# One written-out order exchanged for another: same transfers, other engines for the copies, more 64 by 64 transposes, half the zero products

## The chip, the cores and the metric

The kernel runs on one core of a Trainium2 chip. The metric is the device time of one execution in microseconds (us). TensorE (PE in the profile) multiplies matrices and transposes; its weight loads have a row of their own (PEld). VectorE (DVE), ScalarE (ACT) and GpSimd (POOL) do the elementwise work, and the queues of SyncE (SP), ScalarE and GpSimd issue the transfers (DMA). Each engine executes its own instructions in program order and waits on semaphores for the others.

## The reference

A retention layer (linear attention with a decay per head) is followed by a WaveMLP-like block. B = 4 batches, H = 8 heads, S = 768 tokens, D = 64, so the model width is 512.

```python
for t in range(S):
    state = gamma[None, :, None, None] * state + np.einsum('bhd,bhe->bhde', k[:, :, t], v[:, :, t])
    y[:, :, t] = scale * np.einsum('bhd,bhde->bhe', q[:, :, t], state)
# x = y with the heads side by side: (B, S, 512)
theta = x @ w_theta
zr, zi = x * cos(theta), x * sin(theta)
u = x + einsum('ts,bsd->btd', w_tok_r, zr) + einsum('ts,bsd->btd', w_tok_i, zi)
out = u + maximum(u @ w_ch, 0)
```

## The kernel before

The work is cut into small named steps, and one list, `ORDER`, says in which order they are emitted. A token such as `ck.7.p` calls step `ck` for unit 7 with engine `p` (`p` GpSimd, `v` VectorE, `a` ScalarE, and for transfers `s` the SP queue, `a` the ACT queue). Each engine gets its instructions in the order of the list; `tc.manual_schedule()` leaves that order alone and adds the semaphores. No planner runs in the kernel.

**Retention, 24 units.** Unit n is one half of the heads (4) in one block of 256 tokens; three blocks make a batch, so units come in pairs and six make a batch. `Lk`, `Lq`, `Lv` load 256 KB each. `ck` casts k to bf16, `cq` or `cqs` casts q or also scales it, `cv` scales v. `Tk` and `Tq` transpose with four 128 by 128 products each into one PSUM bank, and `E` copies the bank out. Their second form, `Tk6`, `Tq6` and `E6`, uses sixteen 64 by 64 products each, writes two PSUM banks (both buffers of tag `tr`) and copies them out in two halves. A third form, `Dk`, is a DMA transpose from the SP queue. `A` makes the scores (sixteen products in 64 by 64 mode), `m` masks them on VectorE, `Y` multiplies them with v. `ST` makes the state's increment, `S0` and `S1` add it up, `SB` casts the state's two halves into a block-diagonal tile, and `I` multiplies it with q. `XB` (a cast on any engine) or `XA` (a product with the decay, on VectorE) brings the result out, depending on whether q was scaled before.

**The block after it, 24 tiles of 128 tokens.** `Tx` and `Ex` (or `Tx6` and `Ex6`, or the DMA transpose `Dx`) turn x back. `Hh` multiplies with w_theta, `CN` takes cosine or sine on ScalarE, `z` multiplies both with x. `Tw` and `Ew` (or `Tw6`, `Ew6`) transpose the token weights, whose rows `Pw` loads from the GpSimd queue in three groups for each of the two matrices (`Pw.1.1` is the second group of w_tok_i, rows 128 to 383). `M.t.s` is one pair of products of 512 columns of output tile t, `u` adds x, `Tu`, `Tu6` or `Du` transposes, `O` multiplies with w_ch, `f` closes, `SO` stores. `Mh`, `uh`, `Tuh`, `Euh`, `Oh`, `fh` are the last tile in halves.

**Zero products and constants.** `Z.n` is two products of 128 by 512 on a zero tile into a spare PSUM bank; nothing reads them, and n only makes the token unique. `const1` clears that tile on VectorE, `const6` clears the block-diagonal tiles, `const2`, `const4`, `const5`, `constA` set up positions, identity and mask on GpSimd, `const3`, `const8`, `const9` make the decay tables on ScalarE, `const7` switches its table to sine.

The lines where the two kinds of transpose differ:

```python
for x in range(4):                                      # kq_half: L318
    nc.tensor.transpose(st["kq_ps", n][:, 4 * w + x, :],
                        st["kqb", n][:, w, x * P:(x + 1) * P], K["ident"])
...
for c in range(2):                                      # tiles64: L337
    for r in range(2):
        rows = slice(r * D, (r + 1) * D)
        nc.tensor.transpose(ps[r][c * D:(c + 1) * D, x, :],
                            src[rows, x * P + c * D:x * P + (c + 1) * D],
                            K["ident"][rows, rows])
```

Of the kernel before, what the change touches and what calls it, by code (L numbers as in the profile page):

```python
# [32 lines left out]
Ex.2.v S0.5.v z.0.p Tq.6 E.6.a CN.2.0 cv.6.p Hh.3 SB.5.0.v Tx.3 Tw.1.0 z.1.v SB.5.1.a Ew.1.0.v Ex.3.a
CN.2.1 A.6 I.5 Y.5 ST.6 XA.5.0 z.2.v Tw.0.0 CN.3.0 Tx.4 CN.3.1 Ew.0.0.v S0.6.v XA.5.1 Ex.4.v Hh.4 CN.4.0
CN.4.1 Tw.0.1 M.0.1 Pw.1.1 z.3.v M.0.0 Tw.0.2 Pw.1.2 Ew.0.2.a SB.6.1.a Hh.5 z.4.p SB.6.0.p Lk.9.a M.0.3
ck.7.p cqs.7.p M.0.2 CN.5.1 CN.5.0 cq.8.v m.6 Ew.0.1.v Tw.1.1 Tw.1.2 Ew.1.1.v Lv.9.s M.0.4 M.1.0 Tx.5
Ew.1.2.v M.1.1 S1.6 Tk.7 M.1.4 Pch Ex.5.v z.5.v cv.7.v Tq.8 Tq.7 M.1.2 E.7.a M.0.5 I.6 Y.6 ST.7 A.7
ck.8.a u.0 S0.7.v m.7 XA.6.1 SB.7.1.a M.1.5 M.1.3 XA.6.0 Tw.1.3 M.2.5 Pw.0.2 M.2.3 u.1 S1.7 Tk.8 M.2.1
M.2.0 SB.7.0.v Ew.1.3.a Tu.0 I.7 cv.8.v E.8.a Lk.10.s cv.9.p Y.7 ST.8 A.8 cqs.9.v ck.9.v M.2.4 Du.1
Eu.0.a XB.7.1.a XB.7.0.v S0.8.v SB.8.0.v M.2.2 Tx.6 Tq.9 Tk.9 Lv.10.a ck.10.p cv.10.p Lq.10.s S1.8 u.2  # L40
m.8 O.0 E.9.a SB.8.1.a Hh.6 Tw.1.4 I.8 Y.8 A.9 CN.6.0 Du.2 Lq.14.s CN.6.1 Ex.6.v f.0 ST.9 Tw.0.3 Hh.7
Ew.1.4.v Ew.0.3.a S0.9.v Tw.0.4 M.3.0 CN.7.0 CN.7.1 M.3.2 Dx.7 M.3.1 M.3.5 M.3.3 Lv.11.s Lk.11.s XA.8.1
Ew.0.4.v Lq.11.s M.3.4 S1.9 u.3 Tw.0.5 Tk.10 M.4.5 cqs.10.p XA.8.0 m.9 M.4.3 Tq.10 SB.9.1.a SB.9.0.a I.9
O.2 Lq.12.s Lk.12.s E.10.a Lk.15.s Ew.0.5.v Lk.14.s Y.9 ST.10 Tw6.1.5 Ew6.1.5.0.a Ew6.1.5.1.a A.10 z.7.p
Lv.12.s XB.9.1.a XB.9.0.a f.2 M.4.0 O.1 M.4.1 cq.11.a ck.11.p cqs.14.p m.10 f.1 S0.10.v ck.12.v M.4.4
M.4.2 Tu.3 Eu.3.a Dk.11 Dx.9 SB.10.0.a cqs.12.p u.4 Hh.9 z.6.v ck.15.v M.5.0 M.5.4 SB.10.1.p cv.11.p
M.5.2 M.5.3 I.10 M.5.5 M.5.1 Lq.13.a Tu6.4 A.11 Y.10 ck.14.v ST.11 CN.9.1 CN.9.0 SO.0.a Eu6.4.1.a Hh.8
u.5 Eu6.4.0.v S0.11.v XB.10.0.a m.11 Dk.12 Tx.8 O.4 Lv.13.a SB.11.0.a Lq.15.s Lk.13.s XB.10.1.a CN.8.1
Lk.18.a CN.8.0 SB.11.1.p cv.12.p Lq.16.s I.11 Ex.8.v Y.11 Tk6.14 Tq6.14 ST.12 f.4 E6.14.0.v E6.14.1.a
Lv.15.s O.3 z.8.p XA.11.0 XA.11.1 Hh.10 A.12 S0.12.a f.3 z.9.v SB.12.0.v Tx.10 CN.10.1 Dx.11 Ex.10.v  # L50
Lk.16.s Lv.17.s Hh.11 SO.2.s CN.10.0 m.12 S1.12 z.10.v cq.13.v M.6.1 M.6.2 M.6.0 M.6.3 CN.11.0 CN.11.1
M.7.3 SB.12.1.a Lk.17.a ck.13.a M.7.4 M.7.0 M.6.4 Dk.13 M.7.1 z.11.v SO.3.s A.14 Tu6.5 M.6.5 Eu6.5.0.a
Eu6.5.1.a M.7.2 I.12 Lv.14.s u.6 cqs.15.v M.7.5 M.9.3 ck.17.a m.14 SO.4.a Lq.17.s Lq.18.s Lk.21.s
ck.16.a M.9.0 M.9.5 M.9.1 M.9.4 Lq.19.a M.9.2 Du.6 cv.13.v u.7 u.9 Y.12 cv.14.p ST.13 Tk6.15 Tq6.15
E6.15.0.v E6.15.1.v A.13 O.5 XB.12.1.a XB.12.0.a M.8.1 S0.13.a S1.13 M.8.4 M.8.3 SB.13.0.a SB.13.1.p
cq.16.p m.13 I.13 ck.18.a Y.13 ST.14 A.15 M.8.0 f.5 cq.17.v Lv.18.a M.8.5 M.8.2 XA.13.0 XA.13.1 S0.14.v
SB.14.0.p Lv.16.s Hh.13 S1.14 u.8 M.10.1 cv.15.p cv.17.p SB.14.1.p M.10.0 M.10.4 cqs.18.v M.10.5 CN.13.0
CN.13.1 Hh.12 CN.12.1 I.14 m.15 Y.14 CN.12.0 ST.15 S0.15.v XB.14.1.a SB.15.0.a M.10.3 cv.16.v Dk.16
Dk.17 Du.7 Dx.13 M.10.2 Dk.18 O.6 SB.15.1.p XB.14.0.v S1.15 I.15 Y.15 ST.16 Tx6.12 SO.5.a cv.18.p f.6
S0.16.v A.16 M.11.4 cq.19.p SB.16.1.p M.11.1 Lq.21.a Ex6.12.0.a Ex6.12.1.a z.12.p SB.16.0.a Lk.19.s  # L60
Lk.20.s XB.15.0.a u.10 z.13.p XB.15.1.a m.16 O.7 Du.10 I.16 Y.16 Tu6.8 ST.17 f.7 Eu6.8.0.v Eu6.8.1.a
A.17 Hh.15 CN.15.1 CN.15.0 Dx.14 M.11.2 Tx.15 Lv.22.s SO.7.s M.11.0 M.11.5 S0.17.v SB.17.0.p M.11.3
XA.16.1 m.17 XA.16.0 Ex.15.v Hh.14 SB.17.1.p z.15.p ck.21.p ck.19.p I.17 u.11 Tu6.11 A.18 Y.17 ST.18
Eu6.11.1.v S0.18.v XA.17.1 XA.17.0 O.10 SO.1.a S1.18 Lv.19.a CN.14.1 CN.14.0 Dx.16 Lq.20.a f.10 Lq.22.a
SB.18.0.a Hh.17 Eu6.11.0.a SB.18.1.a I.18 Tk.19 Tq.19 CN.17.1 O.8 CN.17.0 m.18 E.19.a Hh.16 z.14.p
Lv.20.s Du.9 f.8 O.11 Y.18 cv.19.p ck.20.a CN.16.1 ST.19 A.19 Tx6.17 CN.16.0 M.12.1 f.11 Ex6.17.0.v
Ex6.17.1.v cq.20.p Lk.22.s Dk.20 M.12.0 S0.19.a M.13.3 M.13.2 XB.18.1.a SB.19.1.p SB.19.0.v M.13.0
z.17.v cqs.21.v XB.18.0.v S1.19 z.16.v m.19 cv.20.v M.12.3 M.12.2 M.13.5 Lv.21.s M.13.1 M.12.4 M.12.5
I.19 M.13.4 Y.19 ST.20 u.12 A.20 Dk.21 XA.19.1 S0.20.v XA.19.0 ck.22.a cq.22.a SB.20.1.p cv.22.p M.14.3
M.14.5 M.14.1 M.14.4 M.14.2 M.14.0 SB.20.0.p u.13 m.20 S1.20 Hh.19 I.20 Y.20 SO.10.s Lq.23.s Lk.23.s  # L70
cv.21.v u.14 A.21 ST.21 CN.19.0 CN.19.1 S0.21.v M.15.3 M.15.5 S1.21 m.21 XA.20.1 Hh.18 CN.18.1 CN.18.0
Dx.18 Dk.22 ck.23.a M.15.4 M.15.2 SB.21.0.p M.15.1 M.15.0 SB.21.1.v Lv.23.s Du.12 Dx.19 XA.20.0 O.9 f.9
I.21 Y.21 A.22 ST.22 M.16.1 cqs.23.p u.15 m.22 S0.22.v z.18.p z.19.p M.16.5 SB.22.0.p M.16.4 O.12 M.16.0
SO.8.a M.16.2 M.16.3 SB.22.1.p XB.21.0.a XB.21.1.a SO.11.s Du.14 cv.23.p Dk.23 f.12 Du.13 Dx.20 Dx.21
Hh.21 u.16 I.22 A.23 Y.22 ST.23 CN.21.0 CN.21.1 Hh.20 CN.20.1 S0.23.v XA.22.1 XA.22.0 SB.23.0.a M.17.1
M.17.3 CN.20.0 M.17.0 SB.23.1.p I.23 M.17.2 m.23 Y.23 O.13 M.17.4 z.21.v M.17.5 Mh.0.1 Mh.0.3 XB.23.1.v
f.13 Hh.23 u.17 XB.23.0.a SO.13.a CN.23.1 Du.16 Hh.22 z.20.v CN.22.1 Mh.0.2 M.19.3 Dx.23 CN.23.0 Dx.22
# [628 lines left out]
```

## Time and profile before

| | us |
|---|---|
| median of three runs | 164.74 (164.14 to 164.97) |
| span of the profiled execution, first to last instruction | 163.3 |
| TensorE busy | 154.7 (95%) |
| VectorE busy | 114.5 (70%) |
| ScalarE busy | 78.8 (48%) |
| GpSimd busy | 74.3 (45%) |

The profiled execution is known by its span; the device time of the runs also holds what lies before the first and after the last instruction, here 1.4 us between the span and the median. Busy times are sums over the span. TensorE's products are pipelined: one of 512 columns is listed with 380 ns, and the next starts 216 ns after it, so starts are read rather than durations.

### The profile page before, as it was taken

To read this page: it belongs to the slowest core of one execution; us is meant where nothing else is said; L and a number is where in the kernel's file an instruction comes from. 1 tells how busy PE (TensorE), PEld (TensorE's weight loads), DVE (VectorE), ACT (ScalarE), POOL (GpSimd) and SP (SyncE) were. 2 spreads that over 40 slices of the span, in tenths; PEclk is the share of its full clock that TensorE was granted. 3 is DMA by queue.
4 is the path that set the end of the run, shared out by engine and by line. 5 is a ranking of instruction groups with operands and counts; after the bars stand their busy time and mean duration, and the time that the engine had idled before them with its cause. 6 is when DMAs were issued, how large, how long until landed. Compare 5 with 4: busy or idle time off the path is not lost.

```text
span 163.3 us, 5070 instructions
## 1 busy us (share of the span) xinstructions
PE 154.7 (95%) x2100; PEld 85.5 (52%) x2100; DVE 114.5 (70%) x217; ACT 78.8 (48%) x147; POOL 74.3 (45%) x106
## 2 busy tenths in 40 slices
...
DMA  4999999999999999999999999999896527514446
GB/s 116 297 290 252 258 294 240 277 220 285 226 162 275 296 205 220 251 207 245 335 236 172 242 195 305 222 192 276 185 251 129 101 64 225 161 68 128 128 156 230
DMA packets 70118, 35.19 MB, mean 215 GB/s; under 512 B 27472, under 2 KB 67152, under 8 KB 70096
## 3 DMA queue, kind: packets, MB, share of 16 engines
...
q0 software_dynamic: 2688, 3.41, 12.1%
...
## 4 chain that ended last, share of the span: by engine, by line
PE 79%; DMA 7%; DVE 6%; POOL 4%; issue 1%; ACT 1%; DVEq 0%; POOLq 0%
PE y_ps L559 33%; PE o_ps L595 10%; PE th_ps L511 10%; PE zz L279 5%; PE r_ps L458 4%; PE at_ps L380 4%; DMA x_sb<-xT 4%; DMA kqT<-kqb 3%; PE kq_ps L318 3%; PE w_ps L533 2%; DVE at L389 2%; POOL z L525 2%; PE r_ps L446 2%; PE y_ps L620 2%; PE r_ps L408 1%
## 5 line engine op out<-in xcount | busy, mean ns | idle before, releaser
L559 PE MATMUL y_ps<-z,wtr 128*128 128x512 bf16 x138 | 52.4, 380 | 0.0
L559 PE MATMUL y_ps<-z,wti 128*128 128x512 bf16 x138 | 52.3, 379 | 0.0
L525 POOL TENSOR_TENSOR z<-cs,x_sb 128x1024 bf16<-128x1024 bf16 x12 | 25.5, 2135 | 17.7 <-ACT cs L518 10.8
L389 DVE TENSOR_TENSOR at<-at_ps,mask 128x1024 bf16<-128x1024 f32 x24 | 29.2, 1215 | 0.5 <-PE at_ps L380 0.5
L310 POOL TENSOR_TENSOR vb<-vf,vsc 128x512 bf16<-128x512 f32 x15 | 15.6, 1045 | 21.7 <-ACT sbd L136 11.7
L601 DVE SCALAR_TENSOR_TENSOR ot<-o_ps,u 128x512 f32<-128x512 f32 x22 | 15.1, 688 | 13.6 <-PE o_ps L595 13.5
L511 PE MATMUL th_ps<-wth,xT 128*128 128x512 bf16 x96 | 24.5, 380 | 0.0
L566 DVE TENSOR_TENSOR u<-y_ps,x_sb 128x512 bf16<-128x512 f32 x23 | 15.8, 688 | 10.9 <-PE y_ps L559 10.5
L595 PE MATMUL o_ps<-wch,uT 128*128 128x512 bf16 x88 | 22.6, 380 | 0.0
L518 ACT ACTIVATE cs<-th_ps,halfpi 128x512 bf16<-128x512 f32 x24 | 16.3, 682 | 11.8 <-PE th_ps L511 7.0
L518 ACT ACTIVATE cs<-th_ps,zerob 128x512 bf16<-128x512 f32 x24 | 16.4, 684 | 10.6 <-PE th_ps L511 5.1
L559 PEld LDWEIGHTS <-wtr 128*128 128x128 bf16 x138 | 13.5, 98 | 13.4
L559 PEld LDWEIGHTS <-wti 128*128 128x128 bf16 x138 | 13.5, 98 | 12.7 <-issue 0.4
L138 POOL CAST sbd<-s 64x256 bf16<-64x256 f32 (+1 forms) x20 | 8.4, 418 | 24.3 <-DVE s L426 22.1
L136 ACT COPY kqT<-kq_ps 128x1024 bf16<-128x1024 bf16 (+1 forms) x10 | 9.7, 969 | 9.8 <-PE kq_ps L318 9.5
L511 PEld LDWEIGHTS <-xT 128*128 128x128 bf16 x96 | 8.7, 98 | 8.5
L279 PE MATMUL zz<-zero 128*128 128x512 bf16 x30 | 10.8, 495 | 1.9 <-DVE zero L191 1.9
L595 PEld LDWEIGHTS <-uT 128*128 128x128 bf16 x88 | 8.1, 98 | 8.4 <-issue 0.2
L136 ACT CAST kqb<-kqf 128x512 bf16<-128x512 f32 x16 | 9.6, 620 | 5.5 <-DMA kqf<-in_k_dram 5.4
L458 PE MATMUL r_ps<-at,vb 64*64 64x128 bf16 x384 | 10.0, 221 | 1.6 <-DVE at L389 1.6
L380 PE MATMUL at_ps<-kqT 64*64 64x128 bf16 x384 | 10.0, 220 | 1.1 <-DVE kqT L138 0.6
L476 DVE TENSOR_TENSOR xT<-r_ps,qx 128x256 bf16<-128x256 f32 x22 | 8.7, 417 | 1.8 <-PE r_ps L458 0.8
...
## 6 DMA issues: line engine op xcount, KB each, us to landing
vf<-in_v_dram SPq DMA_DIRECT2D x20, 256.0 KB, 5.7
kqf<-in_k_dram SPq DMA_DIRECT2D x19, 256.0 KB, 5.4
kqf<-in_q_dram SPq DMA_DIRECT2D x17, 256.0 KB, 5.7
out_dram<-ot ACTq DMA_DIRECT2D x12, 256.0 KB, 2.5
out_dram<-ot SPq DMA_DIRECT2D x11, 256.0 KB, 2.4
kqf<-in_q_dram ACTq DMA_DIRECT2D x7, 256.0 KB, 5.4
kqf<-in_k_dram ACTq DMA_DIRECT2D x5, 256.0 KB, 6.7
vf<-in_v_dram ACTq DMA_DIRECT2D x4, 256.0 KB, 5.7
```

The costliest lines, as they stand in the source:

```text
L136: nc.scalar.copy(dst, src)
L279: nc.tensor.matmul(t[:m, :cols], K["zero"][:, :m], K["zero"][:, :cols], start=True, stop=True)
L310: engines[e].tensor_mul(in_blocks(vb), by_token(raw["vf", n]), _bcast_last(K["vsc"][:, i, :, h * HU:(h + 1) * HU], D))
L380: nc.tensor.matmul(at_ps[cols, g, j, a, :], kq_at(n, 0, a, j, c)[rows], kq_at(n, 1, slice(0, 2), j, c)[rows], start=(j == 0 and a == 0), s ...
L389: nc.vector.tensor_mul(at.rearrange("p g j a t -> p (g j) (a t)"), st["at_ps", n].rearrange("p g j a t -> p (g j) (a t)"), _bcast_mid(K["m ...
L458: nc.tensor.matmul(st["R", n + 1][c][g * D:(g + 1) * D, j * P:(j + 1) * P], st["vb", n][rows, lo:lo + D], st["at", n][rows, g, j, a, :], s ...
L511: nc.tensor.matmul(th_ps, st["xT", C][:, j, :], K["wth"][:, j, :], start=(j == 0), stop=(j == 3))
L518: nc.scalar.activation(st["cs", C][:, w, :], st["th_ps", C], AF.Sin, bias=K["zerob" if w else "halfpi"], scale=1.0)
L525: engines[e].tensor_mul(st["z", b][:, c], st["cs", C], _bcast_mid(x_of(C), 2))
L559: nc.tensor.matmul(st["y", t], K["wT"][r][:, s0, t0 * P:(t0 + 1) * P], st["z", b][:, s0, r, :], start=(done == 0 and r == 0), stop=(done = ...
L566: nc.vector.tensor_add(st["u", t], st["y", t], st["x", b][:, t0, :])
L595: nc.tensor.matmul(o_ps, st["uT", t][:, j, :], K["wch"][:, j, :], start=(j == 0), stop=(j == nD - 1))
```

## The change

Only `ORDER` is exchanged; no function and no tile is changed. All transfers (`Lk`, `Lq`, `Lv`, `Pth`, `Pch`, `Pw`, `Dk`, `Dx`, `Du`, `SO`, `SOh`) stand in the same order in both lists, on the same queues. The constants' order and the place of every compute step between the transfers are new. Of the steps that may run on several engines, many name another one: of the 24 `z`, GpSimd had 12 and has 3 now. In the second form instead of the first are now `Tk`/`Tq` of units 0, 1, 2, 8 and 19, `Tw.0.3`, `Tw.1.4`, `Tx.8` and `Tx.15` with their copies. Units 7, 10, 14 and 18 go from `cqs` with `XB` to `cq` with `XA`, units 4, 11 and 16 the other way. The list held 15 `Z` and holds 8.

```diff
-const2 Lv.0.s const1 const6.v Z.29 Z.2 const5 Z.38 Lk.0.a const3 Z.35 Z.8 Lq.0.s Lv.1.s Z.28 constA
-const4 Lq.1.a const9 Lk.1.s Z.39 const8 ck.0.p Tk.0 ck.1.a cqs.0.v cv.0.v Tq.0 E.0.v Lq.4.a ST.0 Lk.4.a
-cqs.1.p Tq.1 Lq.2.s S0.0.v SB.0.1.v A.0 Lk.2.s SB.0.0.p cv.1.p Lv.2.s S1.0 Z.15 I.0 Z.27 m.0 Tk.1 E.1.a
-cqs.2.v Z.34 cv.2.p Y.0 ST.1 XB.0.1.a S0.1.v S1.1 SB.1.0.a Pth Lq.3.s Z.18 XB.0.0.v Tq.2 A.1 SB.1.1.a
-ck.2.a I.1 m.1 Y.1 ST.2 Tk.2 const7 Z.23 XB.1.0.v Lk.3.s E.2.v XB.1.1.v A.2 ck.3.p S0.2.v m.2 S1.2
-SB.2.1.a Z.11 cqs.3.p Tq.3 Lv.3.s Tx.0 Tk.3 Z.3 ck.4.p Lv.4.s Lk.5.s Lq.5.s Lv.5.s Lq.6.s Lk.6.s Lv.6.s
-Lq.7.s E.3.a SB.2.0.v I.2 Y.2 XB.2.1.a Ex.0.a cv.3.v cq.4.p Tk.4 Lq.8.s A.3 ST.3 Lk.7.s S0.3.v SB.3.0.a
-S1.3 Lv.7.s Lk.8.s Tx.1 Tq.4 SB.3.1.p cv.4.p m.3 Pw.1.0 XB.2.0.a Ex.1.a I.3 Lv.8.s E.4.a ck.5.a cq.5.a
-Y.3 Pw.0.0 ST.4 Hh.0 S0.4.v XB.3.0.v XB.3.1.v cv.5.v CN.0.1 A.4 CN.0.0 Tq.5 Hh.1 Tk.5 SB.4.0.p SB.4.1.a
-Pw.0.1 Hh.2 m.4 E.5.v I.4 Y.4 ST.5 ck.6.a Tk.6 Tx.2 cq.6.a CN.1.1 CN.1.0 XA.4.1 A.5 XA.4.0 m.5 Lq.9.s
...
+const4 const5 const1 Lv.0.s const2 Z.703 Z.204 Lk.0.a const3 Lq.0.s Z.312 ck.0.v cv.0.v constA Lv.1.s
+cqs.0.p const6.v Tk6.0 Z.855 const8 Lq.1.a ST.0 S0.0.a Tq6.0 E6.0.1.v SB.0.0.v SB.0.1.a cv.1.p Z.748
+Lk.1.s E6.0.0.v ck.1.v Lq.4.a A.0 S1.0 const9 Lk.4.a cqs.1.v Lq.2.s Lk.2.s Tq6.1 m.0 Tk6.1 E6.1.1.a I.0
+Y.0 ST.1 E6.1.0.v S0.1.v A.1 cqs.2.p Lv.2.s SB.1.0.a ck.2.p XB.0.1.a Tq6.2 cv.2.p Pth Lq.3.s Tk6.2
+XB.0.0.v Lk.3.s cqs.3.p SB.1.1.v S1.1 E6.2.1.a m.1 Z.282 cqs.4.v Lv.3.s I.1 Lv.4.s ck.4.a Lk.5.s cv.3.p
+Y.1 E6.2.0.a Lq.5.s ST.2 A.2 Lv.5.s ck.3.a S0.2.v Tq.3 Lq.6.s XB.1.0.v SB.2.0.a Z.700 Tk.3 S1.2 XB.1.1.a
+SB.2.1.a Lk.6.s Lv.6.s m.2 Lq.7.s Tk.4 Tq.4 I.2 E.3.a Y.2 E.4.v ST.3 S0.3.v Lq.8.s SB.3.0.p Lk.7.s Tx.1
+S1.3 A.3 XB.2.0.v XB.2.1.a const7 SB.3.1.p Lv.7.s Tx.0 Lk.8.s I.3 Ex.1.v m.3 ck.5.a cv.4.v Hh.0 Pw.1.0
+Y.3 Lv.8.s cq.5.v ST.4 S0.4.v A.4 Hh.1 SB.4.0.p CN.0.0 Pw.0.0 Tk.5 Ex.0.a cv.5.p SB.4.1.v XB.3.0.a
+CN.0.1 CN.1.0 XB.3.1.v CN.1.1 Pw.0.1 m.4 Tq.5 E.5.v Tx.2 I.4 Ex.2.a ck.6.p Hh.2 z.0.v cq.6.a Y.4 ST.5
+A.5 S0.5.v Tw.1.0 SB.5.0.p XB.4.0.a Hh.3 m.5 SB.5.1.p XB.4.1.a Lq.9.s Tq.6 Ew.1.0.a Tk.6 I.5 CN.3.0
+Pw.1.1 z.1.v E.6.v Y.5 CN.2.1 CN.2.0 CN.3.1 XA.5.0 Tw.0.0 Tx.3 cv.6.p Ex.3.a z.2.v A.6 ST.6 Hh.4 S0.6.a
...
```

103 lines of the change are left out of this document (51 added, 52 removed).

## The prediction

> **What bounds the kernel now.** I read the page first, then busy times by stage, then TensorE's waits, and last starts in the timeline and the chain of waits.
>
> ```profile
> span 163.3 us, 5070 instructions
> ...
> PE 154.7 (95%) x2100; PEld 85.5 (52%) x2100; DVE 114.5 (70%) x217; ACT 78.8 (48%) x147; POOL 74.3 (45%) x106
> ...
> DMA  4999999999999999999999999999896527514446
> ```
> ```profile
> 0.00:7.82 7.82, 5.90 (x15) 2.09 (x16) 2.86 (x8) 5.71 (x10) 5.23 (x34) 1.00 0.79 203
> 7.82:22.15 14.33, 11.49 (x275) 7.79 (x274) 10.74 (x21) 9.88 (x20) 8.41 (x12) 1.00 1.19 271
> 22.15:35.68 13.53, 13.29 (x201) 7.96 (x197) 12.11 (x24) 12.26 (x22) 8.16 (x9) 1.00 1.17 255
> 35.68:64.90 29.22, 28.73 (x419) 17.23 (x418) 22.68 (x46) 16.40 (x29) 15.13 (x16) 1.00 1.15 238
> 64.90:103.00 38.10, 37.98 (x654) 20.46 (x654) 31.23 (x59) 18.37 (x42) 19.66 (x22) 1.00 1.20 245
> 103.00:130.00 27.00, 26.95 (x362) 14.20 (x363) 20.18 (x38) 10.90 (x20) 13.46 (x15) 1.00 0.95 188
> 130.00:160.00 30.00, 30.00 (x184) 15.72 (x181) 14.24 (x25) 5.27 (x11) 4.20 (x2) 1.00 0.48 140
> ```
>
> Each stage's row gives its length, then the busy times of PE, PEld, DVE, ACT and POOL, the granted clock, the share of the DMA engines and GB/s. From 35.68 to 160 TensorE is busy 123.66 of 124.32 us: there only less work on TensorE helps. Before 22.15 it is not full, and the DMA engines are (1.19 in the second row).
>
> ```profile
> PE r_ps L458 <- DVE at L389: 1.6, 2, 1.1
> PE at_ps L380 <- DVE kqT L138: 0.6, 2, 0.4
> PE at_ps L380 <- DMA kqT<-kqb: 0.5, 1, 0.5
> ...
> PE kq_ps L318 <- POOL kqb L138: 0.2, 1, 0.2
> ```
> ```profile
> 35.67 0.67 PEld L533 LDWEIGHTS <-row 128*128 128x128 bf16 x12 [0.38 <-DMA row<-in_moe_w_tok_i_dram]
> ```
>
> The last row is the place that I build on: at 35.67 TensorE's weight load for `Tw.1.1` waits for the rows of w_tok_i (`Pw.1.1`). After it two waits of note are left, the third and fourth row of TensorE's list: 0.5 us for a DMA transpose and 0.2 us for a cast on GpSimd.
>
> **Prices.** Starts, from the chain of waits (start, length, what):
>
> ```profile
> 1.92 6.06 PE zz L279 x14
> ...
> 10.28 0.43 PE zz L279 x2
> 10.71 0.22 PE kq_ps L318 x4
> ...
> 51.03 0.34 PE w_ps L533 x6
> ...
> 68.29 0.25 PE kq_ps L337 x32
> ```
> ```profile
> 40.42 0.40 PE L380 MATMUL at_ps<-kqT 64*64 64x128 bf16 x16
> 40.75 0.39 PE L559 MATMUL y_ps<-z,wtr 128*128 128x512 bf16 x1
> ...
> 49.20 0.39 PE L380 MATMUL at_ps<-kqT 64*64 64x128 bf16 x16
> 49.43 0.29 PE L408 MATMUL r_ps<-vb,kqb 64*64 64x64 bf16 x16
> ```
>
> A product of 512 columns costs 0.43 us in the first stretch and 0.216 us later. Four 128 by 128 transposes cost 0.22 us (0.056 each), six 0.34, and 32 of 64 by 64 cost 0.25 us (0.0078 each), so sixteen cost 0.125. The scores take 0.23 us when 64 by 64 work follows (49.20 to 49.43) and 0.33 us when a full product follows (40.42 to 40.75): a change of mode costs 0.10 us.
>
> **The change, on TensorE.** Counted over both lists: 7 `Z` fewer are 14 products at 0.216, -3.0 us. Ten groups `Tk`/`Tq` and two `Tx` exchange 0.22 for 0.125, two `Tw` exchange 0.34 for 24 x 0.0078 = 0.19: -12 x 0.097 - 2 x 0.15 = -1.45 us. Changes of mode fall from 68 to 64: -0.4 us. In all 4.9 us less of some 147.8.
>
> Most of that lies where it cannot count. Adding up each list at these prices, 25.95 us of TensorE work stands ahead of `Tw.1.1` before and 21.56 after; behind it stand 121.83 and 121.36. What is saved ahead of it shortens the end only if the rows land earlier. Behind it: four `Tk`/`Tq` groups -0.39, two `Tw` -0.30, fewer `Tx` -0.42, one `M` pair that now comes later +0.43, two more changes of mode +0.2. **First term: -0.47 us.**
>
> **The start.** When do the rows land now?
>
> ```profile
> 5.09 0.29 POOL masks.py:199 TENSOR_SCALAR_AFFINE_SELECT ident<-ident 128x128 bf16<-128x128 bf16 x1
> ...
> 15.88 1.17 POOL L138 CAST kqb<-kqf 128x512 bf16<-128x512 f32 x2 [0.82 <-DMA kqf<-in_k_dram]
> ...
> 27.65 1.53 POOL L181 DMA_DIRECT2D row<-in_moe_w_tok_i_dram  x2
> ```
> ```profile
> 1.76 0.44 ACTq L156 DMA_DIRECT2D kqf<-in_q_dram  x1
> ...
> 9.85 1.21 DVE L389 TENSOR_TENSOR at<-at_ps,mask 128x1024 bf16<-128x1024 f32 x1
> ...
> 15.97 0.42 PE L380 MATMUL at_ps<-kqT 64*64 64x128 bf16 x16 [0.39 <-DVE kqT L138]
> ```
> ```profile
> kqf<-in_q_dram ACTq DMA_DIRECT2D x7, 256.0 KB, 5.4
> ```
>
> `const4` and `const5` now stand ahead of `const2` on GpSimd, and `Lq.1.a` stands behind `const8`, which needs `constA`. GpSimd runs the same four steps first; the last of them, now `constA`, ends where the identity ended, near 5.4 us. So `Lq.1` is issued there instead of at 1.76 and, with the queue's median of 5.4 us, lands between 10 and 10.8; `cqs.1.v` stands ahead of `m.0` on VectorE, which so starts at 10.5 to 11.5 us instead of 9.85. This is taken up later: `ck.4.a` waits for its load (landed at 15.88 before) on ScalarE, ahead of `E6.2.0.a`, and after these two copies of 0.6 us `A.2` starts near 17.1 (15.97 before). From there to `Tw.1.1` the new list holds 15.87 us for TensorE; with 1 to 2 us of waits (mask, `cv.4` behind `m.3` on VectorE, first rows) it arrives at 34 to 35. The rows: `Pw.1.1` stands on GpSimd behind `SB.5`, which needs `ST.5`, hence the load of v for unit 5, in the same transfer order. I put its issue at 27 to 28 (27.65 before) and its landing at 35.6, give or take 1. **Second term: 0**, bounds -1 (earlier issue, lighter GpSimd) and +1 (rows later).
>
> **The other engines, behind that point.** Adding the list's steps at the durations of their rows, GpSimd loses 14 us and VectorE gains 5, mainly by nine `z`:
>
> ```profile
> L525 POOL TENSOR_TENSOR z<-cs,x_sb 128x1024 bf16<-128x1024 bf16 x12 | 25.5, 2135 | 17.7 <-ACT cs L518 10.8 <-DVE z L525 4.7 <-DMA x_sb<-xT 2.0
> ...
> L136 ACT COPY kqT<-kq_ps 128x1024 bf16<-128x1024 bf16 x9 | 9.1, 1011 | 9.5 <-PE kq_ps L318 9.5
> L525 DVE TENSOR_TENSOR z<-cs,x_sb 128x1024 bf16<-128x1024 bf16 x12 | 8.9, 738 | 1.3 <-DMA x_sb<-xT 1.2
> ...
> L136 ACT COPY kqT<-kq_ps 128x512 bf16<-128x512 bf16 x1 | 0.6, 585 | 0.3 <-PE kq_ps L337 0.3
> ```
>
> The second form of a transpose is copied out in two halves, 2 x 0.585 instead of 1.01 us on ScalarE, and holds both `tr` banks until then: 0.16 us each on engines that have room, counted in their loads. VectorE is 70% busy. Its tightest stretch is `A.16` to `M.12.0`, where the new list gives it 15.3 us beside 15.0 of TensorE, before taking off that its instructions overlap by some 0.07 each; were that cover gone, 0.3 us would show. What goes: the wait for the casts `ck.19`, `cq.19`, which stood behind a `z` of 2.1 us on GpSimd (0.3 us with the pipeline's restart), and part of the wait at `A.11`:
>
> ```profile
> 59.39 5.47 DMA kqT<-kqb
> ...
> 99.75 1.38 POOL z L525
> ...
> 101.82 1.18 POOL kqb L138 x2
> ```
>
> `Dk.11` takes 5.47 us and left 0.5 us open. In the new list its last input, `ck.11.a`, stands 5.5 us of TensorE work ahead of `A.11`, so about as tight. What is late next: `ck.13.a` stands 4.9 us ahead of `A.13`, and `cq.20.p` follows `z.14`, `cv.19` and `ck.20` on GpSimd ahead of `A.20`; each may cost 0.5. Transfers issue in the old order, so nothing is moved past a queue, but a late input to one `Dk` holds the loads behind it on SP. **Third term: -0.4 us**, bounds -1.0 (no wait left) and +1.5 (three of 0.5). The last tile's chain (`M.20.5`, `u.20`, `Tu.20`, `Eu.20`, `Oa`, `fa`, `fh`) has the same steps with the same distances: 0.
>
> Sum: -0.47 + 0 - 0.4 = -0.9 us on the profiled 163.3. The median of the runs is 1.4 us above that span, which I carry over: 164.74 - 0.9 = 163.8 us.
>
> [...] The first fourteen zero products ran back to back for 5.5 us before the pace went from 0.43 to 0.216. The new list has six of them, a gap until k of unit 0 is cast, then single ones between short groups. [...]
>
> **Rivals.** (1) Slower: the pace stays slow in the start. Up to `A.2` the chain waits for loads and hides it. From 17.1 on 3.5 us of TensorE work lead to `Hh.0` and 12.4 more to `Tw.1.1`; if 5.5 us must again be dense before the pace rises, 2.75 us are lost there. 1 us is cover ahead of the rows, and `S0.4` and `S0.5` come later by as much, so the rows too: +1.7, 165.5 us (bounds 164.6 and 166.4). It decides if products of 512 columns still start 0.43 apart at 17 us. For it: 2.6 us of zeros at the start instead of 6. Against: sparse work between 5.6 and 9 us may do.
> (2) The content does not matter: rows land at the same time and new waits for the DMA transposes (`A.13`, `A.20`, half a us each) take back what is saved: 164.7, bounds 164.2 and 165.0. For it: `Dk` transposes took 5.47 us where inputs now come 4.9 to 5.5 ahead.
> (3) Better: the start is done earlier on GpSimd and the rows land 1 us sooner, with no wait left: -0.47 - 1.0 - 0.4 = 162.9.
>
> **How the numbers follow.** Runs of this kernel lie within 0.4% of their median; 0.5%, 0.8 us, is about what a measurement tells from no change, so faster is below 163.9 and slower above 165.6. Forecast 163.8 (163.2 to 164.2): 0.37. Rival 1: 0.30, half of it above 165.6. Rival 2: 0.20. Rival 3: 0.10. The rest, several new waits in the middle, 0.03, is slower. Faster: 0.32 of the forecast's share and rival 3, 0.42. Slower: 0.15 + 0.03, raised to 0.24 because rival 1's loss also delays every load issued behind a wait. Same: 0.34. The range runs from rival 3 to rival 1's upper part: 162.7 to 166.2.
>
> **What would show it.** Right: `Tw.1.1` starts at 34.6 to 36.6 after a wait for the rows; from there to the end about 124 us with TensorE full; 64 by 64 groups of 32 in 0.25 us; no wait of TensorE on GpSimd's casts. Wrong: products of 512 columns 0.43 apart after 17 us, or `Tw.1.1` past 37, or waits for `kqT` above 1.5 us in all, or TensorE waiting for a `z` on VectorE between `A.16` and `M.12.0`.

## The result, and the profile after

The changed kernel takes 170.69 us (median of four runs, 169.65 to 171.19) where the list before takes 164.48 beside it: a ratio of 1.038, 95% interval 1.033 to 1.042. Slower by 6 us, outside the forecast range. The profiled run took 169.65 us, its span is 167.9. A profile in what follows is one run; the runs of the changed order and its variants scatter mostly by 1 to 4 us (one by 7), those of the old list by 1 to 2, so a profile shows a mechanism and the medians and ratios carry the verdict. Four of the profiles used below (`start_mended`, `all_mended`, `old_head64`, `all_mended_128`) are of runs 1 to 2% longer than the fastest of their kernel; the ratios leave such runs out.

The page of the changed kernel: busy time by engine, the granted clock in 40 slices, and from the list of DMA queues the one that carries instructions:

```profile
span 167.9 us, 5412 instructions
...
PE 153.8 (92%) x2266; PEld 84.7 (50%) x2266; DVE 122.5 (73%) x226; ACT 76.4 (45%) x149; POOL 61.0 (36%) x104
...
PEclk9999599999999999999999999999999999999999
...
q8 instruction: 17, 0.28, 0.7%
```

TensorE has less busy time than before (153.8, not 154.7) in a span that is 4.6 us longer. It issues 166 products more, and in the fifth slice its clock is halved. The busy times by stage, cut where the same steps start as in the table of before (`Hh.0` at 23.23, `Tw.1.1` at 38.03):

```profile
0.00:8.81 8.81, 5.81 (x59) 1.89 (x59) 3.53 (x12) 4.93 (x10) 6.03 (x34) 1.00 0.82 211
8.81:23.23 14.42, 10.16 (x264) 7.66 (x265) 11.67 (x21) 8.57 (x17) 6.73 (x9) 0.88 1.20 268
23.23:38.03 14.80, 13.61 (x226) 8.29 (x223) 13.21 (x24) 13.91 (x27) 10.97 (x15) 1.00 1.17 264
38.03:67.09 29.06, 28.73 (x496) 17.05 (x500) 21.55 (x40) 13.85 (x26) 9.82 (x14) 1.00 1.12 213
67.09:104.00 36.91, 36.20 (x655) 19.30 (x644) 30.12 (x58) 20.40 (x45) 16.97 (x19) 1.00 1.22 248
104.00:132.00 28.00, 27.11 (x403) 13.89 (x400) 24.28 (x45) 8.87 (x19) 10.09 (x13) 1.00 0.91 187
132.00:165.00 33.00, 32.19 (x196) 16.60 (x190) 18.15 (x31) 5.86 (x11) 0.40 (x1) 1.00 0.51 135
```

In the second row TensorE works 10.16 of 14.42 us, part of that at half clock (0.88 in the mean). The column of the granted clock reads 1.00 also where the profile has no record of it: the first record of the full clock is at 14.05 us here and at 7.75 before, and up to there products of 512 columns start 0.40 to 0.43 us apart. The start is at the slow pace twice as long as before. From `Tw.1.1` on it is idle for 126.97 - 124.23 = 2.7 us, where before it was 0.66. And `Tw.1.1` itself, TensorE's weight loads in order of time:

```profile
38.02 0.34 PEld L534 LDWEIGHTS <-row 128*128 128x128 bf16 x6 [0.91 <-DMA row<-in_moe_w_tok_i_dram]
```

It still waits for the rows, but at 38.02 instead of 35.67. So the profile splits the 4.6 us: **2.35 us ahead of `Tw.1.1`, 2.25 behind it** (from there to the end of the span 129.9 us, before 127.6). TensorE's waits (total, times, longest), the long ones:

```profile
PE kq_ps L338 <- DVE kqb L139: 1.7, 1, 1.7
PE kq_ps L338 <- DVE kqb L305: 1.4, 1, 1.4
...
PE r_ps L409 <- issue: 0.9, 1, 0.9
...
PE o_ps L596 <- DMA uT<-u: 0.8, 1, 0.8
...
PE r_ps L447 <- DVE sbd L139: 0.6, 1, 0.6
...
PE th_ps L512 <- ACT cs L519: 0.3, 1, 0.3
```

The first two are the start's waits for casts. The third has no releaser at all. The last three lie in the body, one each at `O.17`, `I.19` and `Hh.14`.

### The profile page after: what moved, and what is told of

It is laid out like the page before. It is cut to its first block, busy times and chain, and to the rows that moved or that the text cites. A ratio compares the mean times of both kernels' runs of the same rounds, so it can differ in the third digit from the quotient of the medians.

```text
span 167.9 us, 5412 instructions
## 1 busy us (share of the span) xinstructions
PE 153.8 (92%) x2266; PEld 84.7 (50%) x2266; DVE 122.5 (73%) x226; ACT 76.4 (45%) x149; POOL 61.0 (36%) x104
## 2 busy tenths in 40 slices
DMA packets 70119, 35.20 MB, mean 210 GB/s; under 512 B 27472, under 2 KB 67152, under 8 KB 70096
## 3 DMA queue, kind: packets, MB, share of 16 engines
q10 hardware_dynamic: 10320, 7.47, 16.3%
q0 software_dynamic: 2688, 3.41, 12.2%
## 4 chain that ended last, share of the span: by engine, by line
PE 64%; DMA 13%; DVE 12%; issue 4%; POOL 2%; ACT 2%; ACTq 0%; SPq 0%; DVEq 0%; POOLq 0%
PE y_ps L560 28%; PE o_ps L596 10%; PE th_ps L512 9%; DMA kqT<-kqb 4%; DMA row<-in_moe_w_tok_r_dram 4%; PE r_ps L459 3%; DMA uT<-u 3%; DMA kqf<-in_q_dram 3%; PE at_ps L381 3%; DVE z L526 2%; DVE at L390 2%; PE r_ps L447 2%; PE kq_ps L319 2%; PE r_ps L409 2%; PE y_ps L621 1%
## 5 line engine op out<-in xcount | busy, mean ns | idle before, releaser
L139 POOL CAST sbd<-s 64x256 bf16<-64x256 f32 (+1 forms) x20 | 7.5, 375 | 44.3 <-DVE s L427 26.1
L311 POOL TENSOR_TENSOR vb<-vf,vsc 128x512 bf16<-128x512 f32 x18 | 18.7, 1040 | 9.2 <-DMA vf<-in_v_dram 9.0
L519 ACT ACTIVATE cs<-th_ps,zerob 128x512 bf16<-128x512 f32 x24 | 16.5, 686 | 12.1 <-PE th_ps L512 8.4
L560 PEld LDWEIGHTS <-wti 128*128 128x128 bf16 x138 | 13.5, 98 | 13.1 <-issue 1.2
L560 PEld LDWEIGHTS <-wtr 128*128 128x128 bf16 x138 | 13.5, 98 | 12.7
L526 DVE TENSOR_TENSOR z<-cs,x_sb 128x1024 bf16<-128x1024 bf16 x21 | 15.4, 739 | 4.7 <-ACT cs L519 2.6
L139 POOL CAST kqb<-kqf 128x512 bf16<-128x512 f32 x16 | 11.8, 747 | 9.3 <-PE u_ps L338 2.7
L137 ACT CAST sbd<-s 64x256 bf16<-64x256 f32 (+1 forms) x20 | 7.4, 371 | 13.2 <-DVE s L427 10.3
L477 DVE TENSOR_TENSOR xT<-r_ps,qx 128x256 bf16<-128x256 f32 x24 | 9.4, 416 | 3.2 <-PE r_ps L409 3.1
L381 PE MATMUL at_ps<-kqT 64*64 64x128 bf16 x384 | 10.9, 231 | 0.5 <-DMA kqT<-kqb 0.3
L305 POOL TENSOR_TENSOR kqb<-kqf,qsc 128x512 bf16<-128x512 f32 x7 | 7.7, 1106 | 6.6 <-DMA kqf<-in_q_dram 6.6
```

The costliest lines, as they stand in the source:

```text
L139: engines[e].tensor_copy(dst, src)
L311: engines[e].tensor_mul(in_blocks(vb), by_token(raw["vf", n]), _bcast_last(K["vsc"][:, i, :, h * HU:(h + 1) * HU], D))
L381: nc.tensor.matmul(at_ps[cols, g, j, a, :], kq_at(n, 0, a, j, c)[rows], kq_at(n, 1, slice(0, 2), j, c)[rows], start=(j == 0 and a == 0), s ...
L519: nc.scalar.activation(st["cs", C][:, w, :], st["th_ps", C], AF.Sin, bias=K["zerob" if w else "halfpi"], scale=1.0)
L526: engines[e].tensor_mul(st["z", b][:, c], st["cs", C], _bcast_mid(x_of(C), 2))
L560: nc.tensor.matmul(st["y", t], K["wT"][r][:, s0, t0 * P:(t0 + 1) * P], st["z", b][:, s0, r, :], start=(done == 0 and r == 0), stop=(done = ...
```

## The experiments

Each median stands beside the list of before on the same chip, 164.27 to 164.63 us in the five sets. "Behind" is the time from the first product of `Tw.1.1` to the end of the span of the profiled run.

### Is the loss in the start, in the body, or both?

`head_before_body_after`: the old order up to `Tw.1.1`, then what is left of the new one. `head_after_body_before`: the reverse.

> The list of before up to the weight load Tw.1.1, then the steps of the changed list that are left, in their order (unit 7 keeps the scaled cast). Theory S+B (the loss has two parts that add: about 1.9 us in the start, about 2.75 us behind Tw.1.1): Tw.1.1 at 35.7 us as before, then the body's loss alone, 164.5 - 0.5 + 2.75 = 166.8 us. Rival (the waits of the body follow from the late start, which shifts the work against the transfers): they go with the old start, 164.0 us.

> The changed list up to Tw.1.1, then the steps of the list of before that are left, in their order. Theory S+B: Tw.1.1 at 38.0 us as in the changed kernel, 2.35 us later than before, and no more is lost behind it: 164.5 + 2.35 = 166.8 us. Rival (the start does not matter, since the body has slack that takes it up, or the body's waits come with the late start): 165 us or less, or 169 and more.

The first: 168.64 us (166.78 to 170.46), `Tw.1.1` at 35.77 as in the list before, 130.7 us behind it. The second: 169.96 us (167.26 to 171.02), `Tw.1.1` at 37.13, 128.5 behind. So both halves lose time of their own, and the body loses it with the old start too: the first rival falls. What a late start costs the old body is less clear. The median of the second run, 169.96, lies where its rival put it (169 or more), while its profile, of a run of 167.26 us, shows 0.9 us lost behind `Tw.1.1`. The two losses add to more than 6 us, so they are not simply additive, and neither run came near the 166.8 us of theory S+B.

### The zero products and the load of q

```diff
 # more_zeros: seven Z more, 15 in all
-Lq.0.s Z.312 ck.0.v ... cv.1.p Z.748 Lk.1.s ... I.1 ... ST.2 A.2
+Lq.0.s Z.312 Z.901 Z.902 ck.0.v ... cv.1.p Z.748 Z.903 Lk.1.s ... I.1 Z.904 Z.905 ... ST.2 Z.906 Z.907 A.2
 # early_q1
-const3 Lq.0.s ... const8 Lq.1.a ST.0
+const3 Lq.1.a Lq.0.s ... const8 ST.0
```

> The changed list with seven more zero products, 15 in all as before: two more at the head, one ahead of the scores of unit 0, four between I.1 and A.2 where TensorE was 35% busy in the window of 14.05 to 17.47 us. Theory 1 (too few zero products: the clock stays slow to 14.05 us and again from 17.47 to 20.88): products of 512 columns are 0.216 us apart from about 8 us on and stay so, the 2.7 us of work from 18.2 to 20.9 halve, Tw.1.1 comes 1 to 1.3 us earlier: 169.5 us. Theory 2 (the late load of q for unit 1 and the late issues of the token weights' rows set the start): Tw.1.1 stays within 0.3 us of 38.0, 170.7 us.

> The changed list with one step moved: the load of q for unit 1 is issued on ScalarE's queue directly behind const3, ahead of const8 and its wait for the constants on GpSimd. Theory 2: it is issued near 2 us instead of 5.23, lands near 7 to 8 instead of 9.76, cqs.1 and the mask of unit 0 follow 1.5 us earlier, and A.2 comes at about 16.2 instead of 17.6: Tw.1.1 1.0 to 1.4 us earlier, 169.4 us. Theory 1: the loads of units 2 to 4 and the slow clock set A.2 and what follows, within 0.4 us of 170.7.

> The list of before with eight zero products instead of 15, three of them at the head as in the changed list, nothing else. Theory 1 (too few zeros cost time by the clock): products of 512 columns stay 0.43 us apart beyond 10 us or fall back to it in a window that was left partly idle, and the kernel is 1 to 1.7 us slower, 165.5 to 166 us. Rival (loads set the pace of the start, so the zeros are free and so is their absence): 164.4, within 0.5 us.

`old_list_half_zeros` drops `Z.35`, `Z.8`, `Z.28`, `Z.39`, `Z.27`, `Z.18`, `Z.11` from the list of before. It takes 165.45 us, ratio 1.007 (1.004 to 1.010), 0.8 us more by the medians and 1.2 by the ratio: `Tw.1.1` at 36.72, and 127.7 behind it as before. Its zero products in order of time:

```profile
9.61 1.03 PE L279 MATMUL zz<-zero 128*128 128x512 bf16 x2
11.07 1.06 PE L279 MATMUL zz<-zero 128*128 128x512 bf16 x2
16.07 0.59 PE L279 MATMUL zz<-zero 128*128 128x512 bf16 x2
```

A pair takes 1.03 to 1.06 us up to 11 and 0.59 at 16, where in before it takes 0.59 to 0.60 from 9.56 on: the slow pace lasts longer without the dense head. That is the price of half the zeros by itself. `more_zeros` takes 168.59 us, 2.1 less than the changed kernel; yet in its profile, of a run of 169.69 us, the clock is halved from 11.84 to 18.66 (0.98 in the mean of the run) and `Tw.1.1` lies at 38.3, so the way that theory 1 gave for the gain is not what that run shows, and where the 2.1 us come from stays open. `early_q1` brings `A.2` from 17.62 to 16.23 us and `Tw.1.1` to 37.16, as theory 2 expected of these places, and 170.29 us in all: the 0.9 us are taken back behind it (130.9 instead of 129.9), first by a wait of 1.1 us for the DMA transpose at `A.11`. Theory 2 was right on the chain and wrong on the end.

### Order and engines

The exchanged letters are those of the 113 steps that both lists name in the same form; for `new_list_old_z` nine `z` go back to GpSimd.

> The list of before in its own order, with its own zero products and kinds of transpose; only the engine letter is exchanged in the 113 copies, casts and products that both lists name with the same step and whose letter differs (nine z from GpSimd to VectorE among them). Theory E (the engines are what costs: VectorE has more to do, and its casts are held while GpSimd runs a product): 2 us or more slower than before, 166.5 to 168 us. Theory O (the order costs: inputs of casts and DMA transposes come too close to their use, whatever the engine): within 0.8 us of 164.4.

> The changed list in its order, with its zero products and kinds of transpose; the same 113 letters are those of the list before. Theory E: the body's loss goes, 170.7 - 2.75 = 168 us or less. Theory O: no better than the changed kernel, 170 us or more, since each order has its letters fitted to it and the foreign ones add waits.

> The changed list with the 24 z on the engines that they had before: twelve on GpSimd instead of three, nine letters exchanged and nothing else. VectorE loses nine products of 0.74 us. If VectorE's load is what the body pays for: 1 us or more faster than the changed kernel, 169.5 us or less. If the holding beside GpSimd's two-operand products is (each z on GpSimd is such a product, 2.1 us long): slower than the changed kernel, 171.5 us or more. If neither: 170.7 within 0.6.

Both exchanges cost more than any theory allowed: 191.56 us (ratio 1.162) and 193.74 us (1.159). So order and engines cannot be priced one without the other: each order has its letters fitted to it. `new_list_old_z`, the nine `z` alone, takes 175.66 us. Two of its waits tell why:

```profile
PE r_ps L409 <- POOL vb L311: 2.6, 2, 2.3
PE r_ps L447 <- POOL sbd L139: 2.1, 3, 1.1
```

The casts that stand behind a `z` in GpSimd's order come late. In the new order VectorE is the better place for these `z`. Whether its load costs the body anything besides, this run cannot tell.

### VectorE held beside GpSimd

In the profile of the changed kernel some casts took several times their usual length. The groups of `SB`'s casts of 64 by 128 on VectorE (busy time, mean ns of one, idle before), first of before, then of after:

```profile
L138 DVE CAST sbd<-s 64x128 bf16<-64x128 f32 x4 | 0.8, 211 | 0.0
```
```profile
L139 DVE CAST sbd<-s 64x128 bf16<-64x128 f32 x4 | 3.6, 893 | 0.1
```

One of them, `SB.19.1`, with the product `cv.22` that GpSimd runs beside it, in order of time:

```profile
113.61 1.03 POOL L311 TENSOR_TENSOR vb<-vf,vsc 128x512 bf16<-128x512 f32 x1
...
113.70 1.03 DVE L139 CAST sbd<-s 64x128 bf16<-64x128 f32 x1
```

The cast ends 0.09 us after the product does. `sb_scalar` moves three such casts:

```diff
-SB.1.1.v ... SB.12.0.v ... SB.19.1.v
+SB.1.1.a ... SB.12.0.a ... SB.19.1.a
```

> The changed list with three letters exchanged: the state's casts SB.1.1, SB.12.0 and SB.19.1 go from VectorE, where each lay beside a product on GpSimd and took 1.03 to 1.44 us instead of 0.21, to ScalarE. Theory H (what costs is that VectorE is held beside GpSimd's two-operand products): these three take 0.3 to 0.4 us; the mask of unit 1 starts 0.9 us earlier and I.19 no longer waits (0.75 us): 170.7 - 0.75 to -1.6, about 169.4 us. Rival (the next instruction of VectorE that reads SBUF is held in its place, or another input is late next): 170.2 us or more.

170.42 us, 0.3 less than the changed kernel and inside the scatter: that is where the rival put it. At the same place VectorE's next instruction is held instead, `cv.20`, 1.59 us where it took 0.69:

```profile
114.41 1.59 DVE L311 TENSOR_TENSOR vb<-vf,vsc 128x512 bf16<-128x512 f32 x1
```

The wait at `I.19` (0.6 us) is gone and other waits stand close behind. The holding is real; moving the casts does not bring the time back.

### Repairing the named waits

`start_mended` is `more_zeros` and `early_q1` together with `SB.1.1.a`. `body_mended` is:

```diff
-SB.12.0.v ... SO.1.a Hh.15 M.11.0 Ex6.15.1.v ck.19.p CN.15.1 XB.16.0.v CN.15.0 ... SB.19.1.v
+SB.12.0.a ... Hh.15 M.11.0 Ex6.15.1.v ck.19.p CN.15.1 XB.16.0.v CN.15.0 SO.1.a ... SB.19.1.a
-O.17 M.18.5 M.21.4 Mh.0.2 M.18.3
+M.18.5 M.21.4 Mh.0.2 M.18.3 O.17
```

> The changed list with the seven more zero products, the early load of q for unit 1, and SB.1.1 on ScalarE: three edits of the start, nothing behind Tw.1.1. If they add: 168.6 us of the seven zeros alone, less 0.9 for Tw.1.1 as in the run with the early load, 167.7 us, with Tw.1.1 at 36.5 or earlier. Rival (the body takes back what the start gives, as it did with the early load alone: A.11 stays near 67 us and O.17 near 144): 168.6 us or more.

> The changed list with four edits behind Tw.1.1 and the start left as it is: SB.12.0 and SB.19.1 on ScalarE, the store SO.1 behind CN.15.0 in ScalarE's order, O.17 four places later, behind M.18.3. If the waits named in the changed kernel's profile are what the body loses: I.19 -0.75, Hh.14 -0.7, O.17 -1.0, in all 168.3 us. Rival (each has another late input close behind it): 170 us or more.

> The edits of start_mended and body_mended together. If the losses are separate and add: 167.7 - 2.4 = 165.3 us. If an anchor in between (A.11, set by the load of q for unit 11 and its DMA transpose) takes back the start: 166.5 to 167.5 us. If neither set of edits names what costs: 168.5 us or more.

168.47, 169.55 and 168.52 us; ratios to before 1.021 (1.017 to 1.026), 1.029 (1.024 to 1.034) and 1.017 (1.011 to 1.022). The body's edits give 1.1 of the expected 2.4 us; the start's give what the zeros alone gave; together they give hardly more than the start's alone. In the start, the load of q and the cast `SB.1.1` gained nothing beyond the zeros, though they ended waits with a named releaser.

But these three profiles, and those of `sb_scalar`, `early_q1` and `new_list_old_z`, share one thing with the changed kernel's: a stall with the releaser "issue" of 0.7 to 2.1 us ahead of `A.2`. TensorE in the changed kernel, in order of time:

```profile
16.20 0.42 PE L459 MATMUL r_ps<-at,vb 64*64 64x128 bf16 x16 [0.86 <-DVE at L390]
16.42 0.32 PE L409 MATMUL r_ps<-vb,kqb 64*64 64x64 bf16 x15
17.62 0.26 PE L409 MATMUL r_ps<-vb,kqb 64*64 64x64 bf16 x1 [0.88 <-issue]
17.62 0.68 PE L381 MATMUL at_ps<-kqT 64*64 64x128 bf16 x16
18.23 0.61 PE L319 MATMUL kq_ps<-ident,kqb 128*128 128x128 bf16 x4
18.64 1.06 PE L280 MATMUL zz<-zero 128*128 128x512 bf16 x2
```

`ST.2` is sixteen products on the same two tiles. Fifteen run, and the last comes 0.88 us later: no input of its own can be late. After it everything runs at half pace (the pair of zeros at 18.64 takes 1.06 us). In `start_mended` ten zero products more stand ahead, and there the stall lies ten products earlier in `ST.2`, five done and eleven to come:

```profile
15.74 0.28 PE L409 MATMUL r_ps<-vb,kqb 64*64 64x64 bf16 x11 [1.15 <-issue]
```

So it is the count of instructions that meets the stall, not the operation: in each of these kernels 226 of TensorE's instructions other than products have started when it begins, by the trace's records. In the changed kernel they are 223 weight loads, a drain and two semaphore instructions. The trace also lists the packets of the queue of kind instruction. When the first of 16 KB lands, when the 227th of these instructions starts, which is a weight load (the expectations below call it the 226th weight load), and how long after the one before it:

```
                         packet lands   227th instruction   after the 226th
changed kernel              16.32          17.62               1.10
early_q1                    14.56          16.22               1.56
more_zeros                  16.06          17.66               0.26
sb_scalar                   16.03          17.61               2.44
start_mended                14.22          15.74               1.35
body_mended                 16.20          17.58               0.97
all_mended                  14.84          16.29               2.01
head_after_body_before      15.55          16.86               0.28
new_list_old_z              16.18          17.60               1.26
before                      16.14          19.19               0.00
head_before_body_after      16.28          18.75               0.00
```

In these nine kernels with the changed start that load comes 1.3 to 1.7 us after the packet, never sooner. Where the packet landed 1.5 to 2.1 us earlier than in the changed kernel (`early_q1`, `start_mended`, `all_mended`) the load came 1.3 to 1.9 us earlier. In `more_zeros` and `head_after_body_before` TensorE got there late by itself and hardly stood still. With the old start it gets there about 2.5 us or more after the packet, and there is no stall. The changed start has 16 products where the old one has 4 for each transpose of units 0 to 2: 72 products and 72 weight loads more.

### The transposes of units 0 to 2

```diff
 # head128, on the changed list; old_head64 exchanges the forms the other way on the list of before
-Tk6.0 ... Tq6.0 E6.0.1.v ... E6.0.0.v ... Tq6.1 ... Tk6.1 E6.1.1.a ... E6.1.0.v
+Tk.0 ... Tq.0 E.0.v ... Tq.1 ... Tk.1 E.1.a
-Tq6.2 ... Tk6.2 ... E6.2.1.a ... E6.2.0.a
+Tq.2 ... Tk.2 ... E.2.a
```

> The changed list with units 0, 1 and 2 transposed in the first form, four 128 by 128 products each instead of sixteen of 64 by 64, one copy instead of two halves: 72 products and as many weight loads fewer ahead of A.2. Theory I (the stall ahead of A.2 is TensorE's instruction stream, of which a packet of 16 KB lands at 16.3 us): no wait at the 226th weight load, which now comes behind A.2 and after the packet; A.2 0.7 to 1 us earlier, Tw.1.1 at 37.0 to 37.4: 169.8 us. Rival (the stall is a late input of A.2 that the trace does not name, and the first form only adds 0.6 us of transposes): A.2 at 17.6 or later, 170.7 us or more.

> The list of before with units 0, 1 and 2 transposed in the second form, sixteen 64 by 64 products, copied out in two halves on VectorE and ScalarE; nothing else. Theory I: TensorE reaches its 226th weight load some 2 us earlier, ahead of the packet of instructions that landed at 16.1 us, and stands still there until 17.4 or later: 0.5 to 1.5 us slower than before, 165 to 166 us. Rival (the second form is cheaper by 0.097 us a group and its count of instructions does not matter): 164.4 us or up to 0.5 less.

`head128`: **167.66 us, 3.0 less than the changed kernel** (ratio to before 1.021, 1.017 to 1.025). `old_head64`: **168.42 us, 4.0 more than the list of before** (3.5 by the ratio, 1.021, 1.017 to 1.026). About half of the loss of 6 us appears and disappears with these three units' transposes, in both orders, in the direction of theory I and by more than it said. The halved copies that belong to the second form were exchanged with the products, so no run prices the two apart. `head128` at the place of the stall:

```profile
16.41 0.32 PE L408 MATMUL r_ps<-vb,kqb 64*64 64x64 bf16 x14
...
16.57 0.39 PE L380 MATMUL at_ps<-kqT 64*64 64x128 bf16 x15
16.89 0.40 PE L318 MATMUL kq_ps<-ident,kqb 128*128 128x128 bf16 x4
17.34 0.38 PE L279 MATMUL zz<-zero 128*128 128x512 bf16 x1
...
35.20 0.34 PEld L533 LDWEIGHTS <-row 128*128 128x128 bf16 x6 [0.66 <-DMA row<-in_moe_w_tok_i_dram]
```

No stall, `A.2` at 16.5, `Tw.1.1` at 35.20. The two other kernels with this start, `head128_loads` and `all128`, have it at 36.28 and 35.93; three with the changed start as it was (the changed kernel, `head_after_body_before`, `body_mended`) at 37.13 to 38.53. And `old_head64`, with the packet landed at 16.14:

```profile
15.80 0.20 PE L337 MATMUL kq_ps<-ident,kqb 64*64 64x64 bf16 x4
17.47 0.28 PE L337 MATMUL kq_ps<-ident,kqb 64*64 64x64 bf16 x11 [1.47 <-issue]
...
20.42 1.06 PE L279 MATMUL zz<-zero 128*128 128x512 bf16 x2
...
39.84 0.67 PEld L533 LDWEIGHTS <-row 128*128 128x128 bf16 x12 [0.78 <-DMA row<-in_moe_w_tok_i_dram]
```

Here the stall stands in the middle of `Tk6.2`'s sixteen products, five done, eleven to come, 1.33 us after the packet. The clock records are halved from 19.37 to 22.78, after a window in which TensorE was busy 52% of the time. `Pw.1.1` is issued at 31.36 instead of 27.65, `Tw.1.1` is 4.2 us late, and behind it the list takes 127.5 us, as before (127.6). So this profile shows the chain: four times the instructions, a stall until the packet is in, a window with little work, 3.4 us at half clock, late units 4 and 5, late casts on GpSimd, late issue and landing of the rows. That the packet is what ends the stall is inferred.

> The changed list with all the transposes that it had put into the second form back in the first: units 0, 1, 2, 8 and 19, Tw.0.3, Tw.1.4, Tx.8, Tx.15. TensorE has 1.45 us more of products, by the prediction's prices. Theory I for the whole kernel (64 by 64 groups run TensorE out of instructions): faster than the changed kernel by 0.5 to 1.5 us, 169.2 to 170.2. Rival (cheaper transposes pay in the body, and only order and engines cost): 171 us or more.

> The edits of the start and of the body together with the first form for units 0 to 2. If theory I holds and the stall at the 226th weight load (1.8 us in the profile of all_mended) goes with nothing in its place: 168.5 - 1.5 = 167 us, Tw.1.1 at 36.5. If the rows of the token weights, issued by GpSimd, set Tw.1.1 anyway: 168 us or more, with waits for the rows.

`all128` takes 168.76 us, 1.1 more than `head128`: in the body the second form seems to pay about what the prices said (units 8 and 19, two `Tw` and two `Tx`: 0.39 + 0.30 + 0.19 = 0.9), though the two intervals overlap a little (1.024 to 1.031 and 1.017 to 1.025). So theory I does not reach into the body. `all_mended_128` takes 169.70 us, worse than `head128` without the edits. In its profile `Hh.0` waits 2.0 us for w_theta, which lands at 23.59 instead of 20.29, `Pth` being issued 1.8 us later on GpSimd: it stands behind `cv.2`, whose load lands at 13.3 instead of 11.5. With the early load of q alone (`early_q1`) `Pth` is issued as late, at 14.37.

### What is left behind `Tw.1.1`

`head128` keeps 3.2 us of the loss. In its profile, of a run of 169.47 us, `Tw.1.1` is ahead of before, but 132.6 us lie behind it (129.9 in the changed kernel), so that this run shows the gain at `Tw.1.1` and then gives it back; the gain of 3.0 us is one of medians. The largest wait is at `A.11`, and the DMA engines have moved 12.9 MB by 55 us where before it was 13.7. Five loads stand in SP's queue behind `Du.1`.

```diff
 # head128_loads on head128, old_loads on the list of before: the same edit
-Du.1 ... Lq.10.s ... Du.2 ... Lq.14.s ... Dx.7 ... Lv.11.s ... Lk.11.s ... Lq.11.s
+Lq.10.s Lq.14.s Lv.11.s Lk.11.s Lq.11.s Du.1 ... Du.2 ... Dx.7
```

> The kernel of head128, with five loads (Lq.10, Lq.14, Lv.11, Lk.11, Lq.11) moved ahead of Du.1 in SP's queue. Theory Q (the queue behind Du.1 is what the body loses first): the loads are issued from 40 us on instead of 46.7 to 55, 13.7 MB or more are moved by 55 us, A.11 no longer waits (2.4 us in the profile of head128) and starts before 66 us: 166 us, 1 to 2 us less than head128's 167.7. Rival (the DMA engines are the limit whatever the order, or Du.1 and Du.2 now come late for O.1 and O.2): 167.4 us or more.

> The list of before with the same five loads moved ahead of Du.1, nothing else. Theory Q: before waits 0.5 us for the DMA transpose of unit 11 at A.11, which goes: 163.9 to 164.2 us, a little less than before. Rival: Du.1 and Du.2 come 2 to 3 us later and O.1, O.2 wait: 164.8 us or more.

167.63 and 164.83 us: nothing gained in the one, 0.3% lost in the other (1.0003 to 1.0048). Theory Q falls, though the edit moved the loads. First `A.11` in `head128`, then, from `head128_loads`, two waits of TensorE that stand there now:

```profile
67.88 0.42 PE L380 MATMUL at_ps<-kqT 64*64 64x128 bf16 x16 [1.98 <-DMA kqT<-kqb]
```
```profile
50.76 0.38 PE L338 MATMUL w_ps<-ident,row 64*64 64x64 bf16 x24 [0.69 <-DMA row<-in_moe_w_tok_r_dram]
...
91.95 0.42 PE L381 MATMUL at_ps<-kqT 64*64 64x128 bf16 x16 [1.10 <-DMA kqT<-kqb]
```

With the loads moved, 13.5 MB are through by 55 us and `A.11` starts at 65.73 without a wait; then `Tw6.0.3` waits for rows, `A.16` 1.10 us for its DMA transpose, `I.19` 0.6 us for its cast, and the end is where it was. What the body loses is not one place. It is several waits, of 0.6 to 2.0 us in these two profiles; where one was taken away, the next took its place. Which property of the new order makes them late together stays open. No version was found that beats the list of before.

## Why the prediction was wrong, step by step

**Where it builds.** Right: `Tw.1.1` waits for rows, and the time splits there. That TensorE is full behind it did not hold for the new list (2.7 us idle).

**First term, TensorE's work behind `Tw.1.1`, -0.47.** In the body the 64 by 64 form saves about what its price says (`all128`, 1.1 us where the prices give 0.9). The term was small, and nothing speaks against it.

**Second term, the start, 0 with bounds -1 and +1.** Here the step failed: measured +2.35 us at `Tw.1.1`. The working up to `A.2` came out: `m.0` at 10.74 (said 10.5 to 11.5), `A.2` at 17.62 (said 17.1). What was missing came at `A.2` itself, a stall and then 3.4 us at half clock. The 64 by 64 transposes were priced by the time of their products alone, 0.125 for 0.223 us. A price for four times the instructions was put at nothing: units 0 to 2 cost 3.0 us in the one order and 3.5 to 4.0 in the other, against a saving of 6 x 0.097 = 0.6. The step "arrives at 34 to 35, rows at 35.6" then fails as a chain: `Hh.0` at 23.23 instead of 22.15, `Pw.1.1` issued at 30.21 instead of 27 to 28, rows at 38.0. The issue is later by more than `Hh.0` is, and that is a second step that failed, the issue "at 27 to 28". From `Hh.0` to it are 6.7 to 7.0 us in the changed kernel, `head128`, `head128_loads` and `all128`, and 5.5 in before and in `old_head64`. In the new order GpSimd's work ahead of `Pw.1.1` hangs on the states of units 4 and 5, which come as late as TensorE makes them, and not on a load: `SB.4` waits 2.09 us for its state, and two `Pw`, `cv.5`, `ck.6` and `SB.5` stand between it and the issue. In the old order `z.0` and `cv.6` stand there. GpSimd in the changed kernel, in order of time:

```profile
25.58 0.51 POOL L139 CAST sbd<-s 64x256 bf16<-64x256 f32 x1 [2.09 <-DVE s L427]
...
30.21 0.72 POOL L182 DMA_DIRECT2D row<-in_moe_w_tok_i_dram  x1
```

The page of before had the row from which to ask, the packets of kind instruction (number, MB, share of 16 engines' span), and the prediction did not read it:

```profile
q8 instruction: 16, 0.26, 0.7%
```

**Third term, the body, -0.4 with bounds -1.0 and +1.5.** Wrong in sign: 129.9 us behind `Tw.1.1` instead of 127.6, which is 2.25 more where the first and third terms together said 0.9 less. The wait for the casts of unit 19 did go. The two risks that were named, `A.13` and `A.20`, did not come; `I.19`, `Hh.14`, `O.17`, `A.16` and, in other runs, `A.11` did. The step that failed is the method: the new places were checked by the distance in TensorE's work between an input and its use, for those inputs that had waited before, and by sums of VectorE's load in one stretch. `O.17` stands 4.5 us of TensorE work behind the end of `u.17` where the old order has 6.9; its DMA transpose took 5.3 us, and 2.6 in the list before. The shorter distance could have been counted ahead, the longer transfer not.

**GpSimd 14 us lighter, VectorE 5 heavier.** GpSimd's busy time fell by 13.3 us, VectorE's rose by 8.0, part of it the held casts. As a price the count was of no use: with nine `z` back on GpSimd the list takes 5 us more, with all letters back 23 more.

**Rival 1, the slow pace.** Its sign and its mark were right: products of 512 columns were still 0.43 apart past 17 us (the pair at 18.64). Its cause was not the zeros alone. Fewer zeros by themselves cost 0.8 to 1.2 us in the old list, where the rival priced the slow pace at 1.7; in the changed kernel the pace had risen at 14.05 and fell again at 17.46, after a window with the waits for the mask and most of the stall in it. The second sign of being wrong, `Tw.1.1` past 37, came too. **Rivals 2 and 3** and the forecast itself are excluded.

Cut into windows of 3.41 us at the clock's records, the trace of the changed kernel has TensorE busy, by its listed products, 2.54, 1.71, 2.19 and 3.02 us of the four windows from 0.40 to 14.05, where the first record of the full clock stands. The next window has 1.20 us, and the clock is halved in the one after it (17.46 to 20.88); that one has 3.26 us, and the clock is full from its end on. In before the two windows up to 7.75, where the full clock is first on record, have 2.42 and 3.42 us; behind it the windows from 11.17 and 17.99 have 2.30 and 2.56 us, and the clock stays full. So in these two traces 0.35 of a window was followed by the half clock and 0.67 was not; that the share of a window decides it is not shown.
